# Four sums at a change of token block placed earlier, the weights' inner sums placed earlier on POOL, and the conversion's places and last two steps rearranged

## The chip, the cores and the metric

The kernel runs on one core of one Trainium2 chip. The metric is the device time of one execution in microseconds, lower is better; the clock of TensorE was granted at 0.997 of full speed over the profiled execution. A core has four engines that compute, each with its own instruction queue worked off in order: TensorE (PE), VectorE (DVE), ScalarE (ACT) and GpSimd (POOL); SyncE (SP) issues nearly all transfers here, also in order.

## The reference

Attention with a hash mask over 4 x 8 heads of 768 tokens, then a feed-forward block over the 3072 tokens:

```python
def _moe_ref(x, w_in, w_out):            # x: 3072 x 512, w_in: 512 x 2048, w_out: 2048 x 512
    h = x @ w_in
    g = h * (1.0 / (1.0 + np.exp(-1.702 * h)))
    return (g @ w_out).astype(np.float32)

# before it: buckets of q and k from the signs of 6 projections, scores masked where the buckets
# differ, softmax, product with v; its output, transposed to tokens x 512, is x
```

The weights come as float64, so the kernel turns them into float32 from their bits.

## The kernel before

The attention fills the first 316 us. The feed-forward block follows in two stages: `w_in` times the tokens (316 to 605 us, lines L737 to L1000), with the activation, and the product with `w_out` (from there to the end, L1069 on). The change touches the first stage and what is done beside it.

Both products save multiplications by Strassen-Winograd's scheme: a 2 x 2 product of blocks takes seven block products, with sums of blocks made beforehand. The helpers `sums_a` (L208, of weights) and `sums_b` (L216, of tokens) each give four sums in an order of their own; the four of `sums_b` are L219 (t1), L220 (the second block becomes a difference, in place), L221 (t2) and L222 (t4). The tokens come in three blocks of 1024 (`sb` = 0, 1, 2), and at each change of block DVE makes these four anew (`x_sums`, from `quarters_x`), into `t_x` and, for L220, into `xT`.

The first stage has 24 steps, eight per block of tokens, each 2 x 128 columns of hidden units against 2 x 512 tokens. Steps 2 to 19 are taken two by two, as pairs 1 to 9 (`NESTED`, L716; `pair_of_steps`, L842). Pair 4 is the first of block 1, pair 8 the first of block 2. In a pair, products 1, 6, 7, 5 and 4 of both steps run as they are ("outer" products, L740, each four PE records of 128x512); p5 uses t1, p6 uses t2, p7 the difference of L220 and p4 t4. Products 2 and 3 are split by the scheme once more (`nested`, L803) into seven "inner" products each, two PE records of 128x256 at L814. They go into two PSUM tiles, `a` and `x`, each with one buffer, so that the next inner product in a tile waits until DVE has added the last (L750, `u<-small` for product 2, `v<-small` for product 3). The six functions `first` to `sixth` (L817 to L836) are called adds 1 to 6 here (add 2 is two instructions). Those of product 3, but for the first, are carried into the next pair (`behind`).

Between the products a pair has ten places, at which the steps listed in `hooks` for it are emitted (`hook`, L893):

| place | after | place | after |
|---|---|---|---|
| 1 | p1 of the first step | 6 | p7 and its corner sum of the first step, add 2 |
| 2 | p1 of the second step | 7 | p7 of the second step, add 3 |
| 3 | p6 of the first step | 8 | p5, corner sum of the second step, add 4 |
| 4 | p6 of the second step | 9 | p4 of the first step, add 5 |
| 5 | p5 of the first step, add 1 | 10 | p4 of the second step, add 6, add 1 of product 3 |

At these places stand, besides the token sums:

- The conversion of a chunk of weights (`convert`, L158, a generator driven by `conversions`, L1117), six steps per chunk: L180, L182, L188 (with ACT's L190), L193, L195, L198. The first reads the chunk from `raw`, which has one buffer; L193 reads it last, and with it the load of the next chunk is emitted on SP (L162). A chunk of `w_out` is written with a stride, since `dst` is four columns of 128 apart. `places_of` gives the six places of the first and of the second step's chunk. The last step of each block (steps 7 and 15) has none, so pairs 3 and 7 have no conversion in their second half.
- POOL's sums of weights that pairs 1 to 3 make for the pairs behind them: `in_sums` (L236, four of 128x512) and `nest_w` (L776, eight of 128x128).
- POOL's sums of token blocks for the inner products (`nest_x`, L790), at places 1 to 4 of pairs 4 and 8.

The finished blocks go to memory by SP (`keep`, L743): c22, c21, u and v after ACT's activation, and POOL makes four sums of them for the second stage first ("outer sums", `g_outer`, L752: L219 to L222 again, on POOL, `t<-v,u` and so on), taken off one after the other by `some` (L766) at several points of a pair.

PE, DVE, ACT and POOL run in the order in which the code emits. SP's order is set by a scheduler at the build.

```python
for i, f in zip((1, 2, 4), x_sums[1:]):
    on(i, f)
places_of = (3, 4, 4, 5, 6, 6), (7, 8, 9, 9, 10, 10)
```

Of the kernel before, what the change touches and what calls it, by code (L numbers as in the profile page):

```python
# [8 lines left out]
F32 = mybir.dt.float32  # L9
# [4 lines left out]
Alu = mybir.AluOpType  # L14
# [24 lines left out]
def kernel(  # L39
# [17 lines left out]
    nc = tc.nc  # L57
# [100 lines left out]
    def convert(cv, dst, src, queue=None, psum=None):  # L158


        raw = cv.tile([P, CW, 2], U32, tag="raw", name="raw")
        (queue or loader[0]).dma_start(out=raw, in_=src)  # L162

        def of(x):
            return x if len(dst.shape) == 2 else x.rearrange("p (x r) -> p x r", r=dst.shape[2])

        lo, hi = raw[:, :, 0], raw[:, :, 1]
        bits = cv.tile([P, CW], U32, tag="bits", name="bits")
        if psum is None:
            part, size = dst.bitcast(U32), hi.bitcast(F32)  # L170
        else:
            part = psum.tile([P, CW], U32, tag="part", name="part")
            size = psum.tile([P, CW], F32, tag="size", name="size")
        yield


        if psum is None:
            nc.vector.scalar_tensor_tensor(part, hi, 3, masks[0x3FFFFFFF], op0=Alu.logical_shift_left, op1=Alu.bitwise_and)
        else:
            nc.vector.tensor_scalar(part, hi, 3, 0x3FFFFFFF, op0=Alu.logical_shift_left, op1=Alu.bitwise_and)  # L180
        yield
        nc.vector.scalar_tensor_tensor(bits, hi, 0xC0000000, part, op0=Alu.bitwise_and, op1=Alu.bitwise_or)  # L182
        yield

        if psum is None:
            nc.vector.tensor_tensor(part, bits, masks[0xFF800000], op=Alu.bitwise_and)
        else:
            nc.vector.tensor_scalar(part, bits, 0xFF800000, None, op0=Alu.bitwise_and)  # L188

        nc.scalar.activation(size, hi.bitcast(F32), Act.Square)  # L190
        part = part.bitcast(F32)
        yield
        nc.vector.scalar_tensor_tensor(part, lo, 2.0**-52, part, op0=Alu.mult, op1=Alu.mult)  # L193
        yield
        nc.vector.tensor_tensor(dst, of(bits.bitcast(F32)), of(part), op=Alu.add)  # L195
        yield

        nc.vector.scalar_tensor_tensor(dst, of(size), (1.125 * 2.0**-15) ** 2, dst, op0=Alu.is_ge, op1=Alu.mult)  # L198

    wi = w_in.bitcast(U32).rearrange("(kc ki) (f two) -> kc ki f two", ki=P, two=2)  # L200
    wo = w_out.bitcast(U32).rearrange("(fc fi) (d two) -> fc fi d two", fi=P, two=2)
# [6 lines left out]
    def sums_a(eng, a11, a12, s3, a22, s1, s2, s4, a21=None):  # L208

        a21 = s3 if a21 is None else a21  # L210
        return [lambda: eng.tensor_tensor(s1, a21, a22, op=Alu.add),
                lambda: eng.tensor_tensor(s3, a11, a21, op=Alu.subtract),
                lambda: eng.tensor_tensor(s2, s1, a11, op=Alu.subtract),
                lambda: eng.tensor_tensor(s4, a12, s2, op=Alu.subtract)]

    def sums_b(eng, b11, b12, b21, b22, t1, t2, t4):  # L216


        return [lambda: eng.tensor_tensor(t1, b12, b11, op=Alu.subtract),  # L219
                lambda: eng.tensor_tensor(b12, b22, b12, op=Alu.subtract),  # L220
                lambda: eng.tensor_tensor(t2, b22, t1, op=Alu.subtract),  # L221
                lambda: eng.tensor_tensor(t4, b21, t2, op=Alu.subtract)]  # L222
# [4 lines left out]
    def quarters_in(cols):  # L227
        w = [w_in_sb[:, K2 * k : K2 * (k + 1), F2 * i + cols.start : F2 * i + cols.stop]
             for i in range(2) for k in range(2)]
        return w + [s_in[:, i, :, cols] for i in range(3)]  # L230

    def quarters_x(sb):
        x = [xT[:, K2 * k : K2 * (k + 1), (2 * sb + j) * XT : (2 * sb + j + 1) * XT] for k in range(2) for j in range(2)]
        return x + [t_x[:, i] for i in range(3)]

    def in_sums(mt, count=1):  # L236
        return sums_a(nc.gpsimd, *quarters_in(slice(mt * P, (mt + count) * P)))
# [45 lines left out]
    def attention(ff):  # L283
# [4 lines left out]
        with actx:  # L288
# [226 lines left out]
            def begin(n):  # L515
                if 0 <= n - 2 < len(in_chunks) - LATE:
                    conv[n] = convert(cv, *in_chunks[n - 2])
                    step(n)
# [176 lines left out]
    def feed_forward(tag, late=()):  # L695
# [9 lines left out]
        with ExitStack() as fctx:  # L705
# [70 lines left out]
            def nest_w(t):  # L776
                sums = []
                m = slice(2 * t * P, (2 * t + 2) * P)
                for o in TWICE:
                    w = quarters_in(m)[LEFT[o]]  # L780
                    x = [w[:, k, i * P : (i + 1) * P] for i in range(2) for k in range(2)]
                    n = 3 if t < 2 else 4
                    new = twice.tile([P, n, P], F32, name=f"w{o}{t}")
                    new = [new[:, i] for i in range(n)]
                    s3 = x[2] if n == 3 else new[3]
                    W[o, t] = [x[0], x[1], s3, x[3]] + new[0:3]
                    sums += sums_a(nc.gpsimd, x[0], x[1], s3, x[3], *new[0:3], a21=x[2])
                return sums

            def nest_x(sb, rooms):  # L790
                sums = {}
                for o in TWICE:
                    b = quarters_x(sb)[RIGHT[o]]
                    b11, b12, b21, b22 = (b[:, k, j * TH : (j + 1) * TH] for k in range(2) for j in range(2))
                    t1, d12, t2, t4 = ([rooms.pop(0)] + [rooms.pop(0) for _ in range(3)])
                    X[o, sb] = [b11, d12, b21, b22, t1, t2, t4]
                    sums[o] = [lambda a=t1, b=b12, c=b11: nc.gpsimd.tensor_tensor(a, b, c, op=Alu.subtract),
                               lambda a=t2, b=b22, c=t1: nc.gpsimd.tensor_tensor(a, b, c, op=Alu.subtract),
                               lambda a=d12, b=b22, c=b12: nc.gpsimd.tensor_tensor(a, b, c, op=Alu.subtract),
                               lambda a=t4, b=b21, c=t2: nc.gpsimd.tensor_tensor(a, b, c, op=Alu.subtract)]  # L800
                return sums
# [248 lines left out]
            def g_sums(n):  # L1050
                return sums_b(nc.vector, *g_quarters(n)) if n < len(steps_out) else [lambda: None] * 4
# [65 lines left out]
            def conversions(cv, psum, chunks):  # L1117


                gens = [convert(cv, *x, psum=psum) for x in chunks]  # L1120
                next(gens[0])
                yield
                for i, x in enumerate(gens):
                    for at in range(6):
                        next(x, None)
                        if at == 3 and i + 1 < len(gens):
                            next(gens[i + 1])
                        yield

            def on(i, *fs):  # L1130
                hooks[i] = hooks.get(i, []) + list(fs)
# [49 lines left out]
            for t in NESTED:  # L1181
                sb, at = divmod(t, MT // 2)
                hooks = {}
                if at == 0:
                    for i, fs in zip((1, 2, 3, 4), (more[2][:2], more[2][2:], more[3][:2], more[3][2:])):
                        on(i, *fs)
                    for i, f in zip((1, 2, 4), x_sums[1:]):
                        on(i, f)
                    places_of = (3, 4, 4, 5, 6, 6), (7, 8, 9, 9, 10, 10)
                else:  # L1190
                    places_of = (1, 2, 2, 3, 3, 4), (6, 7, 7, 7, 9, 9)
                for n, late_by in zip((2 * t, 2 * t + 1), places_of):
                    x = todo.pop(n, [])
                    for i in late_by:
                        on(i, *x[:1])
                        x = x[1:]
                    on(5 if n % 2 == 0 else 10, *x)
                if t + 1 < MT // 2:
                    on(5, *in_sums(2 * t + 2, 2))
                    on(8, *nest_w(t + 1))  # L1200
                elif t + 1 == MT // 2:
                    on(5, *nest_w(0))
                if at == MT // 2 - 1:
                    x_sums = sums_b(nc.vector, *quarters_x(sb + 1))
                    more = nest_x(sb + 1, places[sb + 1])
                    on(10, x_sums[0])
                whole(pair_of_steps(t, hooks))
                yield
            turn[0] = -1
            for n in range(2 * NESTED.stop, 3 * MT):  # L1210
# [11 lines left out]
                t = {3 * MT - 2: g_sums(0)[:2], 3 * MT - 1: g_sums(0)[2:]}.get(n, []) if n > 3 * MT - 3 else []  # L1222
# [61 lines left out]
    def whole(steps):  # L1284
        for _ in steps:
            pass

    ff = feed_forward("", in_chunks[len(in_chunks) - LATE :])
    attention(ff)
    whole(ff)  # L1290
# [42 lines left out]
```

## Time and profile before

| | |
|---|---|
| median of 3 runs | 869.86 us (869.5 to 870.85) |
| the profiled execution | 868.91 us |
| its span | 867.1 us |
| instructions in it | 13723 |
| transfers | 132.12 MB, mean 152 GB/s |

Busy time by stretch of the span, us of each engine:

| stretch, us | PE | DVE | ACT | POOL |
|---|---|---|---|---|
| 300 to 400 | 99.42 | 69.08 | 42.68 | 68.07 |
| 400 to 450 | 47.05 | 36.78 | 18.48 | 32.66 |
| 450 to 500 | 50.00 | 35.45 | 19.93 | 23.68 |
| 500 to 550 | 48.21 | 39.53 | 19.17 | 29.76 |
| 550 to 600 | 50.00 | 32.18 | 18.14 | 41.52 |

A line of a group reads: line of the kernel, engine, operation, out<-in by the program's names, shape, count, then busy us, mean ns of one, and the idle time of the engine ahead of them with what ended it. A line of the waits reads: who waited for whom, us in all, how many times, the longest. A line of the timeline: start and length in us, engine, line, operation, out<-in, shape, count, and in brackets the idle time ahead of it.

### The profile page before, as it was taken

Reading aid. Unit: us, or ns where it says so; the run is one execution under the profiler, and the core shown is the slowest. Engines: PE = TensorE matmul, PEld = TensorE weight load, DVE = VectorE, ACT = ScalarE, POOL = GpSimd, SP = SyncE. Lnnn points to the kernel's source line nnn. Section 1 sums busy time; section 2 is a strip of 40 time slices with the busy share of each in tenths; the row PEclk is TensorE's granted clock in tenths of the full one; section 3 lists DMA queues with packets and bytes.
Section 4 is the critical chain, followed back from the end, with each engine's and each line's share of the span. In section 5 each row is a group of like instructions: output and inputs, shape, how many; then the busy total and the mean of one; then the engine's idle time right before and its main releaser. Section 6 shows DMA issues by size and latency. Waiting matters only on the chain.

```text
span 867.1 us, 13723 instructions
## 1 busy us (share of the span) xinstructions
PE 850.9 (98%) x4953; PEld 517.9 (60%) x4953; DVE 686.4 (79%) x1032; ACT 340.4 (39%) x567; POOL 344.0 (40%) x322
## 2 busy tenths in 40 slices
PE   8999999999999999999899999999999999999996
PEld 4444444444444444555455545544888888888885
DVE  4589999999999884666777668656788977897786
ACT  5866667777666644334344434343000000000000
POOL 4242224334323559667743364779914100000000
PEclk9999999999999999999999999999999999999998
DMA  5635645445552204436565547559754685467524
GB/s 128 99 54 108 106 86 85 85 90 121 101 96 63 62 2 170 169 107 220 183 206 197 202 149 242 195 191 325 259 193 155 201 246 197 164 206 243 195 98 100
DMA packets 169164, 132.12 MB, mean 152 GB/s; under 512 B 123616, under 2 KB 138112, under 8 KB 163712
## 3 DMA queue, kind: packets, MB, share of 16 engines
q1 hardware_dynamic: 166528, 129.70, 52.3%
q10 hardware_dynamic: 2560, 1.46, 0.8%
q8 instruction: 41, 0.67, 0.3%
q14 instruction: 35, 0.29, 0.1%
HBM read 79.69 MB, written 50.33 MB: 150 GB/s over the span
## 4 chain that ended last, share of the span: by engine, by line
PE 91%; DVE 4%; POOL 2%; DMA 1%; issue 1%; SPq 0%; ACT 0%; ACTq 0%; DVEq 0%; POOLq 0%
PE product L1080 27%; PE product L740 22%; PE ps L432 18%; PE av L465 15%; PE small L814 6%; PE dn L486 1%; PE hash L408 1%; DVE xT L1084 1%; DMA q<-in_q_dram 1%; DVE v L750 1%; DVE y L1060 1%; DMA raw<-in_moe_w_out_dram 0%; DVE t_x L221 0%; POOL v L220 0%; POOL t L219 0%
## 5 line engine op out<-in xcount | busy, mean ns | idle before, releaser
L433 ACT ACTIVATE e<-ps 128x768 f32<-128x768 f32 x192 | 151.2, 812 | 25.6 <-PE ps L432 23.1
L432 PE MATMUL ps<-qT,kT 64*128 64x384 f32 x768 | 155.1, 482 | 0.0
L440 POOL TENSOR_TENSOR acc<-e 128x768 f32<-128x768 f32 x32 | 51.8, 1619 | 194.1 <-ACT e L433 174.7
L465 PE MATMUL av<-e,v 128*32 128x385 f32 x1536 | 128.0, 487 | 0.0
L740 PE MATMUL product<-xT,w_in_sb 128*128 128x512 f32 x216 | 100.2, 593 | 0.0
L465 PEld LDWEIGHTS av<-e,v 128*32 128x32 f32 x1536 | 48.5, 109 | 76.3 <-issue 74.0
L740 PE MATMUL product<-t_x,s_in 128*128 128x512 f32 x192 | 89.2, 593 | 4.3 <-DVE t_x L221 4.3
L432 PEld LDWEIGHTS ps<-qT,kT 64*128 64x128 f32 x768 | 68.0, 187 | 38.5 <-issue 38.4
L1093 ACT COPY u<-product 128x256 f32<-128x256 f32 x21 | 7.8, 372 | 171.8 <-PE product L1080 138.5
L219 POOL TENSOR_TENSOR t<-v,u 128x512 f32<-128x512 f32 x24 | 33.4, 1390 | 89.4 <-ACT v L747 84.5
L432 PE MATMUL ps<-qf,kf 64*128 64x384 bf16 x384 | 62.8, 324 | 0.1
L740 PEld LDWEIGHTS product<-xT,w_in_sb 128*128 128x128 f32 x216 | 40.9, 190 | 35.8 <-issue 33.1
L740 PEld LDWEIGHTS product<-t_x,s_in 128*128 128x128 f32 x192 | 36.3, 190 | 35.9 <-issue 33.9
L441 POOL TENSOR_TENSOR acc<-acc,e 128x768 f32<-128x768 f32 x32 | 55.8, 1744 | 2.5
L446 DVE SCALAR_TENSOR_TENSOR acc<-e 128x768 f32<-128x768 f32 x32 | 47.7, 1491 | 5.1 <-ACT e L433 5.1
L740 PE MATMUL product<-t_x,w_in_sb 128*128 128x512 f32 x96 | 45.2, 593 | 0.0
L750 DVE TENSOR_TENSOR v<-small,v 128x256 f32<-128x256 f32 x63 | 26.1, 419 | 23.7 <-PE small L814 23.4
L432 PEld LDWEIGHTS <-kf 64*128 64x128 bf16 x384 | 19.0, 94 | 35.1 <-issue 6.2
L448 DVE TENSOR_TENSOR acc<-acc,e 128x768 f32<-128x768 f32 x32 | 34.3, 1072 | 3.3
L448 DVE TENSOR_TENSOR acc<-acc,acc 128x768 f32<-128x768 f32 x32 | 31.2, 974 | 6.3 <-POOL acc L441 3.2
L1080 PE MATMUL product<-raw_g,xT 128*128 128x256 f32 x152 | 35.1, 379 | 0.0
L750 DVE TENSOR_TENSOR u<-small,u 128x256 f32<-128x256 f32 x63 | 25.5, 417 | 11.1 <-PE small L814 8.0
(243 smaller groups left out, 1643.5 us busy)
## 6 DMA issues: line engine op xcount, KB each, us to landing
raw_g<-g_dram SPq DMA_DIRECT2D x22, 1024.0 KB
s_in<-g_dram SPq DMA_DIRECT2D x20, 1024.0 KB
g_dram<-t SPq DMA_DIRECT2D x72, 256.0 KB
g_dram<-c SPq DMA_DIRECT2D x48, 256.0 KB
raw<-in_moe_w_in_dram SPq DMA_DIRECT2D x16, 512.0 KB
raw<-in_moe_w_out_dram SPq DMA_DIRECT2D x16, 512.0 KB
v<-in_v_dram SPq DMA_DIRECT2D x32, 192.0 KB
g_dram<-u SPq DMA_DIRECT2D x24, 256.0 KB
```

Source lines behind the costliest of these rows:

```text
L219: return [lambda: eng.tensor_tensor(t1, b12, b11, op=Alu.subtract), lambda: eng.tensor_tensor(b12, b22, b12, op=Alu.subtract), lambda: eng ...
L432: nc.tensor.matmul(ps[:, j, 0:HS], a[hs, keys], m[hs, cols], start=not last, stop=last)
L433: nc.scalar.activation(es[c][:, kt, :, 0:HS], ps[:, :, 0:HS], Act.Exp, scale=1.0 / D**0.5)
L440: nc.gpsimd.tensor_tensor(acc, es[c][:, 0, :, 0:HS], es[c][:, 1, :, 0:HS], op=Alu.add)
L441: nc.gpsimd.tensor_tensor(acc, acc, es[c][:, 2, :, 0:HS], op=Alu.add)
L446: nc.vector.scalar_tensor_tensor(acc, e[0], T * TINY, e[1], op0=Alu.add, op1=Alu.add)
L448: nc.vector.tensor_tensor(acc, acc, x, op=Alu.add)
L465: nc.tensor.matmul(av[D * j + d : D * j + d + 32, :], vt[:, t, j, d : d + 32], es[c][:, t, j, :], start=(t == 0), stop=(t == T - 1))
L740: nc.tensor.matmul(ps, wq[LEFT[i]][:, kc, :], xq[RIGHT[i]][:, kc, :], start=(start and kc == 0), stop=(kc == K2 - 1), skip_group_check=not ...
L750: nc.vector.tensor_tensor(dst, x, y, op=Alu.add)
L814: nc.tensor.matmul(ps[at], wq[LEFT[i]], xq[RIGHT[i]], start=start, stop=True, skip_group_check=not start)
L1080: nc.tensor.matmul(ps, wq[LEFT[i]][:, c, :], gq[RIGHT[i]][:, c, :], start=(c == 0), stop=(c == F4 - 1))
```

## The change

In `convert`, for the chunks converted beside the products (those with a PSUM pool): the sum of the two parts is written back into `bits`, in order, and only the last step writes to the destination with its stride. In the pairs:

- Pairs 4 and 8: of the four token sums, L220 and L222 stand at places 1 and 3; L219 and L221 are moved into the pair before, to its places 8 and 10, where L219 alone stood at 10. The conversion's places become (2, 4, 5, 6, 6, 7) and (7, 8, 8, 9, 9, 10).
- All other pairs: the conversion's places become (2, 2, 3, 3, 4, 4) and (6, 7, 7, 8, 9, 9).
- Pairs 2 and 3: POOL's weight sums move from places 5 and 8 to 1 and 3 (pair 3: from 5 to 1). Pair 1 keeps 5 and 8.

```diff
-        nc.vector.tensor_tensor(dst, of(bits.bitcast(F32)), of(part), op=Alu.add)
+        bits = bits.bitcast(F32)
+        whole = bits if psum is not None else dst
+        nc.vector.tensor_tensor(whole, bits if psum is not None else of(bits), part if psum is not None else of(part), op=Alu.add)
         yield
 
-        nc.vector.scalar_tensor_tensor(dst, of(size), (1.125 * 2.0**-15) ** 2, dst, op0=Alu.is_ge, op1=Alu.mult)
+        nc.vector.scalar_tensor_tensor(dst, of(size), (1.125 * 2.0**-15) ** 2, of(whole) if psum is not None else whole,
+                                       op0=Alu.is_ge, op1=Alu.mult)
...
-                    for i, f in zip((1, 2, 4), x_sums[1:]):
+                    for i, f in zip((1, 3), (x_sums[1], x_sums[3])):
                         on(i, f)
-                    places_of = (3, 4, 4, 5, 6, 6), (7, 8, 9, 9, 10, 10)
+                    places_of = (2, 4, 5, 6, 6, 7), (7, 8, 8, 9, 9, 10)
                 else:
-                    places_of = (1, 2, 2, 3, 3, 4), (6, 7, 7, 7, 9, 9)
+                    places_of = (2, 2, 3, 3, 4, 4), (6, 7, 7, 8, 9, 9)
...
                 if t + 1 < MT // 2:
-                    on(5, *in_sums(2 * t + 2, 2))
-                    on(8, *nest_w(t + 1))
+                    on(5 if t == 1 else 1, *in_sums(2 * t + 2, 2))
+                    on(8 if t == 1 else 3, *nest_w(t + 1))
                 elif t + 1 == MT // 2:
-                    on(5, *nest_w(0))
+                    on(1, *nest_w(0))
                 if at == MT // 2 - 1:
                     x_sums = sums_b(nc.vector, *quarters_x(sb + 1))
                     more = nest_x(sb + 1, places[sb + 1])
-                    on(10, x_sums[0])
+                    on(8, x_sums[0])
+                    on(10, x_sums[2])
```

## The prediction

> **What bounds the kernel now.** I read the busy times, then who waits for whom on TensorE (PE), then the timelines at those waits.
>
> ```profile
> PE 850.9 (98%) x4953; PEld 517.9 (60%) x4953; DVE 686.4 (79%) x1032; ACT 340.4 (39%) x567; POOL 344.0 (40%) x322
> ```
>
> PE is busy for 98% and the change takes no matmul away, so only PE's gaps can be won, or new ones lost. All of PE's waits between 316 and 650 us, from the view of waits (total us, times, longest):
>
> ```profile
> PE product L740 <- DVE t_x L221: 4.3, 2, 2.5
> ...
> PE small L814 <- DVE u L750: 0.7, 2, 0.4
> PE small L814 <- DVE v L750: 0.3, 1, 0.3
> ```
>
> The first stands at the two changes of token blocks, pairs 4 and 8. PE's timeline at pair 8, and VectorE's (DVE's) beside it:
>
> ```profile
> 507.49 1.88 PE L740 MATMUL product<-xT,w_in_sb 128*128 128x512 f32 x4
> 509.21 0.59 PE L814 MATMUL small<-xT,w 128*128 128x256 f32 x2
> 511.58 1.95 PE L740 MATMUL product<-t_x,s_in 128*128 128x512 f32 x4 [1.77 <-DVE t_x L221]
> ```
>
> ```profile
> 505.46 1.27 DVE L219 TENSOR_TENSOR t_x<-xT 128x1024 f32<-128x1024 f32 x1
> ...
> 508.04 1.73 DVE L220 TENSOR_TENSOR xT<-xT 128x1024 f32<-128x1024 f32 x1
> ...
> 510.18 1.25 DVE L221 TENSOR_TENSOR t_x<-xT,t_x 128x1024 f32<-128x1024 f32 x1
> ```
>
> Unhindered, an inner product (two records) takes 0.43 us from start to start and an outer one (four) 1.72. p6 should start at 509.21 + 0.43 = 509.64 and starts at 511.58, because t2 (L221) comes out of DVE only at 511.43: 1.94 us lost. At pair 4 the same is 416.04 - 413.37 = 2.67. Behind each a smaller gap follows, since DVE is then late with the inner adds: 425.32 - 424.71 = 0.61 and 520.43 - 520.25 = 0.18. Pair 1's end has two more, 0.46 and 0.45. Nothing else from 316 to 650 us is over 0.15, so 6.31 us are all there is to win.
>
> The other view is what DVE and SyncE's queue (SP) wait for in that stretch:
>
> ```profile
> DVE part L180 <- DMA raw<-in_moe_w_out_dram: 8.8, 6, 3.1
> ```
>
> ```profile
> SPq L744 <- POOL t L219: 69.5, 23, 7.5
> ...
> SPq L744 <- POOL v L220: 29.4, 24, 4.6
> ...
> SPq L744 <- POOL t L221: 20.9, 21, 2.5
> ```
>
> The conversion has one raw buffer: the next load goes out behind L193, which reads it last, and L180 waits for it. Stores of POOL's sums stand ahead of it on SP. The timeline at pair 5 to 6, SP then DVE:
>
> ```profile
> 454.64 0.32 SPq L744 DMA_DIRECT2D g_dram<-t  x1
> 455.99 0.32 SPq L744 DMA_DIRECT2D g_dram<-v  x1
> 457.23 0.32 SPq L744 DMA_DIRECT2D g_dram<-t  x1
> 457.65 0.38 SPq L162 DMA_DIRECT2D raw<-in_moe_w_out_dram  x1
> ```
>
> ```profile
> 462.27 0.70 DVE L180 TENSOR_SCALAR part<-raw 128x512 uint32<-128x512 uint32 x1 [0.57 <-DMA raw<-in_moe_w_out_dram]
> ```
>
> L180 can start 4.62 us after the load's issue. Over the seven loads that it waited for, this is 3.62, 3.73, 4.30, 4.47, 4.62, 4.65 and 5.29.
>
> **The change, part by part.**
>
> *The sums at the change of blocks.* t1 moves from place 10 to 8 of the pair before, t2 from place 2 to place 10, into t1's old slot. That slot (505.46) lies 4.2 us ahead of p6, and t2 takes 1.25 to 1.95 us (its range over pairs 4 and 8), so p6 no longer waits. With it goes the lateness of the adds behind. Gain: 2.67 + 1.94 + 0.61 + 0.18 = 5.40. In its new slot t1 runs 1.27 to 2.29 us (2.29 where it met POOL's sums at pair 4) ahead of an inner add: from 501.55 to at most 503.84, add 0.42, PE's lag 0.15 (520.28 to 520.43): 504.41. PE needs it at 504.48. Hidden by 0.07; each tenth beyond that is a tenth on PE, twice.
>
> *POOL's weight sums.* In pairs 2 and 3 they go ahead of the outer sums: 4 x 1.3 + 8 x 0.46 = 8.9 us into an idle stretch of 14.6 us (360.5 to 375.1, POOL waiting for ScalarE), and 3.7 us into one of 4.88. The outer sums behind end sooner, and so does what SP stores. Nothing on PE; without the idle stretch they would only swap places.
>
> *L195 written in order.*
>
> ```profile
> L198 DVE SCALAR_TENSOR_TENSOR w_out_sb<-size,w_out_sb 128x512 f32<-128x512 f32 x16 | 16.9, 1056 | 0.9
> L195 DVE TENSOR_TENSOR w_out_sb<-bits,part 128x512 f32<-128x512 f32 x16 | 16.9, 1053 | 0.2
> ...
> L193 DVE SCALAR_TENSOR_TENSOR part<-raw,part 128x512 f32<-128x512 uint32 x18 | 12.4, 691 | 0.3
> ```
>
> L195 becomes what L193 is, 0.69 us; L198 still writes with a stride, so it stays at 1.05 (0.69 at best). 16 x 0.36 = 5.8 us less DVE work, which PE hardly waits for: DVE then waits for a load or a product instead.
>
> *Pair 1's conversion.* L193 goes behind the fourth inner add, and L195 is shorter. v, c and add 4 each come 0.6 sooner, so the first gap there (add 5 behind L193, 360.94 against 360.72) is 0.22 instead of 0.46; L195 0.72 after it, L198 1.05, two adds of 0.33: the second is some 0.12 instead of 0.45. Gain 0.57 (0 to 0.91).
>
> *The conversion at pairs 4 and 8.* Here I expect the gain to go. L193 moves from place 5 to 6, L180 of the next chunk stays at 7, so one outer and one inner product lie between them instead of twice that. And in the order of SP's queue as the changed kernel builds it, the load stands on SP behind the stores of t0, v, t2 (POOL's L219, L220, L221) and c22; now it stands ahead of them all. Walking pair 8: p5's sum on DVE 515.98, inner add of v 516.58. In before POOL's L219 starts 1.16 after that add and the store of L221 goes out 3.89 later (519.54, 520.70, 524.59): 521.63. Then c22 and the load, 0.42 to 0.5 each: 522.5 (L193 is done at 521.1, so SP decides). L180: 522.5 + 4.5 = 527.0, taking the two loads with the same stores ahead (4.47, 4.62). Queued behind L180 on DVE are v, c and add 4: 0.60 x 3 + 0.42 + 0.15 = 2.37, so PE may go on at 529.37. It gets there at 529.53 - 1.94 - 0.18 = 527.41. Lost: 1.96. Then L182 and L188, both at place 8 now, stand ahead of add 5: 529.13 + 0.72 + 0.60 + 0.42 + 0.15 = 531.02, PE there at 529.80: 1.22 more. 3.18 per change, 6.36 for two (pair 4 comes to the same within 0.1). With 3.62 for the load it is 2.3 each, 4.6; with 5.29, 3.97 each, 7.9.
>
> [...]
>
> *Sum.* 868.91 (span 867.1 and 1.8 around it) - 5.40 - 0.57 + 6.36 = 869.30, or +0.39. The median of the runs is 869.86, 0.95 above the profiled one; on it, 870.2. Bounds: -5.97 + 4.6 gives 868.5, -5.40 + 7.9 gives 872.4.
>
> **The rivals.**
>
> *The load is in time* (faster). SP would issue it right behind L193 at 521.1 and it would take 3.62: L180 at 524.7, add 4 visible at 527.1, no loss; L182 and L188 still cost 0.93. -5.97 + 1.9: 865.8. For: L193's own time allows it. Against: POOL's sums stand ahead on SP, and SP waits for L219 alone 69.5 us.
>
> *The load is quick, the queue as I walked it.* 3.62 us: 868.5. For: two rows of seven. Against: both had no store of POOL's within 0.4 us ahead. [...]
>
> *The load is slow* (slower). 5.29 at both changes and nothing won at pair 1: 872.4. It decides from about 5 us from issue to L180. For: the row at 530.45, with six stores within 3.3 us ahead. Against: only one of seven.
>
> *p6 still waits.* If t1 and t2 were held in their new slots so that t2 came no sooner, 4.6 us come back: 874.8. Against: t2's new slot has 4.2 us to spare.
>
> **How the numbers follow.** Forecast 0.42; quick load 0.10; in time 0.15; slow 0.28; p6 waiting 0.05. 0.2% is 1.7 us, about what a measurement of this kernel can tell from no change. The likeliest, 870.2, has 868.5 to 872.4 as its own range. The whole range goes down to 865.7, so that the load in time is just inside, and up to 872.6, past the slow load's 872.4; p6 waiting and the halves of the two outer cases that lie beyond their own numbers are left out, some 2 in 10. Faster: 0.15 and a little of the quick loads, 0.17. Slower: 0.28 + 0.05, 0.33. The same: 0.50.
>
> **What would show it.** p6 without a wait for L221 at pairs 4 and 8; L195 at 0.69; in their place PE waiting at L814 for DVE's u, twice at each change, 1 to 3 us and 1.2 us; L180 waiting some 4 us for raw there; on SP the raw load behind t, v, t, c. I am wrong if L180 starts less than 2.5 us behind L198 at these pairs, or if PE's new waits add up to less than 4 or more than 8 us.

## The result, and the profile after

The changed kernel takes 871.36 us (median of 20 runs, 870.19 to 874.98) and the kernel before 870.22 us beside it (20 runs, 868.89 to 871.32). The ratio is 1.0017, with a 95% interval of 1.001 to 1.0025: slower by some 1.5 us, a step that lies at the edge of what was called no change. The forecast was +0.39 us. The profiled execution took 870.98 us, 2.07 more than the one of before.

The page's busy times of the changed kernel:

```profile
PE 853.1 (98%) x4953; PEld 520.4 (60%) x4953; DVE 682.2 (78%) x1032; ACT 340.8 (39%) x567; POOL 346.0 (40%) x322
```

DVE has 4.2 us less to do. PE has the same 4953 records and yet 2.2 us more busy time. Busy time that grows while the work stays the same is the first sign that something other than a wait is at work.

All of PE's waits between 316 and 650 us (who waited for whom; us in all, times, longest):

```profile
PE small L817 <- DVE u L753: 5.7, 4, 1.9
```

The waits for t2 and those for `v` and `u` at pairs 1 and 4 are gone from this view, and four new ones stand in their place. (Three lines were added in `convert`, so L814 is L817 here, L750 is L753, L740 is L743, L219 to L222 are L222 to L225, L195 is L197 and L198 is L200.) PE's timeline at pair 8, where p6 is the `t_x` product of 510.50:

```profile
510.06 0.59 PE L817 MATMUL small<-xT,w 128*128 128x256 f32 x2
510.50 1.88 PE L743 MATMUL product<-t_x,s_in 128*128 128x512 f32 x4
...
526.39 1.88 PE L743 MATMUL product<-t_x,w_in_sb 128*128 128x512 f32 x4
530.17 0.70 PE L817 MATMUL small<-xT,w 128*128 128x256 f32 x2 [1.89 <-DVE u L753]
531.81 0.70 PE L817 MATMUL small<-xT,s_in 128*128 128x256 f32 x2 [0.95 <-DVE u L753]
```

p6 starts 0.44 us after the inner product ahead of it, so it waits for nothing. Later an outer product of 1.72 us should be followed at 528.11 and is followed at 530.17: 2.06 us lost; the next inner product should come 0.53 later and comes after 1.64: 1.11 lost. SP's queue and DVE at the same place:

```profile
521.29 0.32 SPq L747 DMA_DIRECT2D g_dram<-v  x1
522.53 0.32 SPq L747 DMA_DIRECT2D g_dram<-t  x1
522.94 0.38 SPq L747 DMA_DIRECT2D g_dram<-c  x1
523.41 0.41 SPq L162 DMA_DIRECT2D raw<-in_moe_w_out_dram  x1
```

```profile
521.23 0.69 DVE L193 SCALAR_TENSOR_TENSOR part<-raw,part 128x512 f32<-128x512 uint32 x1
...
527.90 0.69 DVE L180 TENSOR_SCALAR part<-raw 128x512 uint32<-128x512 uint32 x1 [3.96 <-DMA raw<-in_moe_w_out_dram]
...
529.70 0.41 DVE L753 TENSOR_TENSOR u<-small,u 128x256 f32<-128x256 f32 x1
530.03 0.68 DVE L182 SCALAR_TENSOR_TENSOR bits<-raw,part 128x512 uint32<-128x512 uint32 x1
530.74 0.69 DVE L188 TENSOR_SCALAR part<-bits 128x512 uint32<-128x512 uint32 x1
531.34 0.41 DVE L753 TENSOR_TENSOR u<-small,u 128x256 f32<-128x256 f32 x1
```

L193 is done with `raw` at 521.92, but the load of the next chunk goes out at 523.41, behind v, t and c. L180 starts 4.49 us after that, and add 4 (the `u` at 529.70) is queued behind L180; PE's next product in that tile, add 6's, waits for it. Then L182 and L188 stand ahead of add 5 (531.34). The product behind it, the first of product 3, waits for that add and starts at 531.81, which ends the second gap. Below, the wait for add 4 is called the first gap, the wait for add 5 the second.

What the waits don't show is in a table of windows around the same place of pair 4 (us, length, then busy us of PE, PEld, DVE, ACT and POOL, PE's granted clock, share of the transfer engines, GB/s):

```profile
430.00:434.00 4.00, 1.14 (x4) 0.40 (x3) 3.96 (x8) 1.79 (x4) 1.27 (x1) 1.00 0.79 301
434.00:436.00 2.00, 2.00 (x5) 1.03 (x6) 1.97 (x5) 1.46 (x3) 0.00 (x0) 0.67 0.82 300
436.00:438.00 2.00, 2.00 (x4) 0.91 (x3) 0.79 (x1) 0.33 (x2) 0.00 (x0) 0.50 0.87 161
438.00:440.00 2.00, 2.00 (x7) 1.18 (x6) 0.85 (x2) 0.43 (x1) 0.00 (x0) 0.97 0.96 370
```

Behind pair 4's two gaps TensorE is granted half its clock for about 3.4 us (from 434.7 to 438.1). The records of an outer product, which start every 0.43 us elsewhere, start every 0.85 us there; summed over the records this loses 1.64 us. Pair 8 shows no such stretch in this execution, and neither does any place between 316 and 650 us in the profile of before.

The stage can now be added up. Gaps on PE before: 6.31 us. After: 0.17 (pair 1) + 2.08 + 1.11 (pair 4) + 2.06 + 1.11 (pair 8) = 6.53. That is +0.22 us, and the half clock's 1.64 makes it +1.86 of the 2.07 by which the two profiled executions differ.

### The profile page after: what moved, and what is told of

It reads as the page before. It is cut to its first block, busy times and chain, and to the rows that moved or that the text cites. A ratio compares the mean times of both kernels' runs of the same rounds, so it can differ in the third digit from the quotient of the medians.

```text
span 869.1 us, 13717 instructions
## 1 busy us (share of the span) xinstructions
PE 853.1 (98%) x4953; PEld 520.4 (60%) x4953; DVE 682.2 (78%) x1032; ACT 340.8 (39%) x567; POOL 346.0 (40%) x322
## 4 chain that ended last, share of the span: by engine, by line
PE 85%; POOL 7%; issue 3%; DVE 3%; DMA 1%; ACT 0%; SPq 0%; ACTq 0%; POOLq 0%; DVEq 0%
PE product L1083 27%; PE product L743 18%; PE ps L435 18%; PE av L468 15%; PE small L817 4%; POOL t L224 1%; PE dn L489 1%; POOL t L222 1%; PE hash L411 1%; POOL v L223 1%; DMA raw<-in_moe_w_out_dram 1%; POOL t L225 1%; DVE xT L1087 1%; PE tp L369 1%; POOL xT L803 1%
## 5 line engine op out<-in xcount | busy, mean ns | idle before, releaser
L743 PE MATMUL product<-xT,w_in_sb 128*128 128x512 f32 x216 | 101.7, 601 | 0.0
L743 PE MATMUL product<-t_x,s_in 128*128 128x512 f32 x192 | 89.1, 592 | 0.0
L222 POOL TENSOR_TENSOR t<-v,u 128x512 f32<-128x512 f32 x24 | 33.3, 1387 | 87.1 <-ACT v L750 87.1
L743 PEld LDWEIGHTS product<-xT,w_in_sb 128*128 128x128 f32 x216 | 41.2, 192 | 36.2 <-issue 33.6
L743 PEld LDWEIGHTS product<-t_x,s_in 128*128 128x128 f32 x192 | 36.5, 190 | 30.9 <-issue 28.9
L753 DVE TENSOR_TENSOR v<-small,v 128x256 f32<-128x256 f32 x63 | 26.4, 421 | 30.7 <-PE small L817 30.5
L743 PE MATMUL product<-t_x,w_in_sb 128*128 128x512 f32 x96 | 45.2, 593 | 0.0
L225 POOL TENSOR_TENSOR t<-c,t 128x512 f32<-128x512 f32 x24 | 33.1, 1378 | 3.9 <-DMA g_dram<-t 2.2
```

Of the source, the lines that this page charges most:

```text
L743: nc.tensor.matmul(ps, wq[LEFT[i]][:, kc, :], xq[RIGHT[i]][:, kc, :], start=(start and kc == 0), stop=(kc == K2 - 1), skip_group_check=not ...
```

## The experiments

The theory after the result: (a) late raw load and the two conversion steps ahead of add 5 cost what the token sums win, and (b) two gaps so close to each other bring the half clock, which makes the rest. The rivals: the loss lies in another part of the change, or the 1.5 us are only further direct waiting. Each kernel was timed beside the kernel before.

**L193 one place earlier at pairs 4 and 8.** Only the place of L193 differs from the changed kernel.

```diff
-                    places_of = (2, 4, 5, 6, 6, 7), (7, 8, 8, 9, 9, 10)
+                    places_of = (2, 4, 5, 5, 6, 7), (7, 8, 8, 9, 9, 10)
```

> The changed kernel, with L193 of the first chunk of pairs 4 and 8 back at place 5 (places 2, 4, 5, 5, 6, 7); all else as changed. Theory A (late load: L193 one place later puts the raw load on SP behind POOL's stores, L180 waits for it, and the inner adds behind L180 hold PE): the load goes out ahead of the stores again, PE's four waits for u (5.7 us by the view of waits, 6.35 by PE's timeline) are gone, and the time is 5.4 to 6 us under the kernel before, a ratio of 0.993 to 0.994. Theory B (besides, the two gaps of each change lie so close that TensorE's clock halves for 3.4 us in some executions, 1.7 us each): no stretch at half clock before the end of the span. Rival C (the loss comes from the moved token sums, POOL's sums or the last two steps of the conversion, not from its places): PE's waits stay and the time is within 1 us of the changed kernel, ratio 1.001 to 1.002.

Measured: 862.54 us (861.59 to 863.54) against 869.74; ratio 0.9913 (0.9898 to 0.9927), some 7.5 us faster, where 5.4 to 6 were expected. SP and DVE at pair 8 in this kernel:

```profile
515.47 0.32 SPq L747 DMA_DIRECT2D g_dram<-t  x1
515.89 0.37 SPq L162 DMA_DIRECT2D raw<-in_moe_w_out_dram  x1
516.88 0.32 SPq L747 DMA_DIRECT2D g_dram<-c  x1
```

```profile
514.39 0.70 DVE L193 SCALAR_TENSOR_TENSOR part<-raw,part 128x512 f32<-128x512 uint32 x1
...
519.92 0.69 DVE L180 TENSOR_SCALAR part<-raw 128x512 uint32<-128x512 uint32 x1 [0.70 <-DMA raw<-in_moe_w_out_dram]
```

The load goes out 0.8 us after L193's end (1.5 in the changed kernel), ahead of c. It still takes 4.03 us to L180, but L193 itself is earlier in its pair, so DVE waits 0.70 us instead of 3.96. PE's gaps in the stage are down to 0.21 and 0.18, both at pair 1; at pairs 4 and 8 there is none. That is 5.92 us less of gaps; the rest is taken up with the clock below. L182 and L188 are where the changed kernel has them: with L180 in time they no longer delay add 5. So the whole loss at these pairs hangs on when `raw` is free and when the load goes out. This version beats both kernels.

**The token sums alone**, in the kernel before.

```diff
-                    for i, f in zip((1, 2, 4), x_sums[1:]):
+                    for i, f in zip((1, 3), (x_sums[1], x_sums[3])):
...
-                    on(10, x_sums[0])
+                    on(8, x_sums[0])
+                    on(10, x_sums[2])
```

> The kernel before with the token sums alone moved (t1 at place 8, t2 at 10 of the pair before, L220 and L222 at 1 and 3). Theory A: p6's two waits and the two small ones behind them are gone, 5.4 us, and nothing takes their place, since L193 stays at place 5; pair 1's 0.9 us stays. 864.5 to 865.5, a ratio of 0.9935 to 0.995. Rival C: the moved sums themselves hold DVE, so PE waits for u or v at the end of pairs 3 and 7 or in pairs 4 and 8, and less than half of the 5.4 us is gained.

Measured: 863.57 us (863.15 to 864.87); ratio 0.9926 (0.9912 to 0.9941), some 6.4 us faster. The waits left on PE in the stage:

```profile
PE small L814 <- DVE u L750: 0.4, 1, 0.4
PE small L814 <- DVE v L750: 0.3, 1, 0.3
```

Both are pair 1's (gaps of 0.55 and 0.46). All four gaps at pairs 4 and 8 are gone, 6.31 to 1.01 = 5.30 us of direct gaps. This one part of the change is worth more than the change as a whole.

**L182 and L188 one place later at pairs 4 and 8**, from the changed kernel.

```diff
-                    places_of = (2, 4, 5, 6, 6, 7), (7, 8, 8, 9, 9, 10)
+                    places_of = (2, 4, 5, 6, 6, 7), (7, 9, 9, 9, 9, 10)
```

> The changed kernel with L182 and L188 of the second chunk of pairs 4 and 8 at place 9 instead of 8 (7, 9, 9, 9, 9, 10), behind add 5. Theory A: the first gap of each change stays at about 2.05 us; the second, 1.11, goes from 0.4 us behind the first to some 2 us later, behind an outer product, at add 6, at about its size. Direct loss as in the changed kernel, 6.3 us. Theory B: with the two gaps further apart fewer executions show a stretch at half clock, the runs spread less than the changed kernel's 870.2 to 875.0, and the median is 0.5 to 1.5 us under it, 870 to 871. Against B: same spread, median within 0.4 us of the changed kernel, 871.0 to 871.8.

Measured: 869.82 us (868.95 to 870.97); ratio 0.9999 (0.999 to 1.0008). PE at pair 4:

```profile
432.82 0.70 PE L817 MATMUL small<-xT,w 128*128 128x256 f32 x2 [1.97 <-DVE u L753]
433.36 0.59 PE L817 MATMUL small<-xT,s_in 128*128 128x256 f32 x2
433.79 1.88 PE L743 MATMUL product<-xT,w_in_sb 128*128 128x512 f32 x4
436.69 0.67 PE L817 MATMUL small<-xT,w 128*128 128x256 f32 x2 [1.01 <-DVE v L753]
```

The second gap hasn't gone, it has moved: from add 5 to the add of `v` behind it, 3.9 us after the first gap's end instead of 1.6. The direct gaps of the stage are even 0.45 us more than in the changed kernel (6.98), and yet the time is lower, 0.9999 against 1.0017 (and 1.0024 in the repeat below). The clock in this profile stays at 1.00 through the stage, and the mean granted clock of its runs is 0.9958 against 0.9947 for the changed kernel. More direct waiting and less time speaks for (b) and against further waiting as the cause.

**The two loads on ScalarE's queue**, from the changed kernel: the raw loads of pairs 4 and 8 no longer queue on SP.

```diff
-                gens = [convert(cv, *x, psum=psum) for x in chunks]
+                gens = [convert(cv, *x, nc.scalar if i in (7, 14) else None, psum) for i, x in enumerate(chunks)]
```

> The changed kernel with two loads alone, those that L180 at place 7 of pairs 4 and 8 waits for, issued from ScalarE's queue instead of SP's; L193 stays at place 6. In the profile of the changed kernel these loads go out 1.5 us after L193's end, behind POOL's stores. If the stores on SP make the load late (theory A, as walked in the prediction), it goes out 0.1 us after L193, L180 starts some 1.5 us sooner and the first gap of each change goes from 2.05 to about 0.5, the second stays near 1.1: 3 us less direct loss, and few stretches at half clock, 867 to 868.5. If L193's own place is what counts and SP's order nothing, the gaps stay and the time is that of the changed kernel.

Measured: 866.63 us (866.13 to 867.59); ratio 0.9961 (0.9947 to 0.9974). At pair 8:

```profile
519.45 0.33 ACTq L162 DMA_DIRECT2D raw<-in_moe_w_out_dram  x1
```

```profile
523.73 0.70 DVE L180 TENSOR_SCALAR part<-raw 128x512 uint32<-128x512 uint32 x1 [2.33 <-DMA raw<-in_moe_w_out_dram]
```

The load goes out at once after L193 (L197 behind it starts at 519.40), 1.5 us sooner than on SP, and takes much the same, 4.28 us. PE's first gap falls from 2.06 to 0.43, at pair 4 from 2.08 to 0.61; the second stays 1.11 at both. So, of some 3.2 us per change, 1.5 to 1.6 is the place of the load behind the stores and 1.1 is the second gap, with L182 and L188 ahead of add 5; that the rest is the load's own length follows from the trace's times and was not tried apart. No half clock shows in the stage.

**Useless products in the gaps**, from the changed kernel. At pairs 4 and 8 PE computes four 128x256 products (`filler(4)`) ahead of add 6's product, where the first gap lies, and two more behind it (`filler(2)`), where the second lies, into a PSUM tile of their own that nobody reads. If the idle time in the gaps is what brings the half clock, it should then stay away, and the kernel should be faster for it.

```diff
...
                 def sixth():
+                    filler(4)
                     add(q12, go(3), q12)
+                    filler(2)
                     done(0)
```

> The changed kernel with six more matmuls in PE's queue at each of pairs 4 and 8: four in front of the inner product at which the first gap lies (add 6's, 2.05 us), two in front of the one with the second (1.11 us). They repeat an inner product into a spare PSUM tile that nobody reads, 0.43 us each, so 1.72 and 0.86 us of the gaps are filled and nothing else is later. [...] Rival (the clock has no part; the changed kernel's excess over the forecast has another cause): the time is that of the changed kernel within 0.4 us, or longer by up to 5 us if the added matmuls do not fit into the gaps.

Measured: 869.95 us (868.43 to 871.5) against 869.56; ratio 1.0003 (0.9994 to 1.0012). PE at pair 4:

```profile
429.15 1.88 PE L743 MATMUL product<-t_x,w_in_sb 128*128 128x512 f32 x4
430.87 1.89 PE L819 MATMUL fill<-xT,w_in_sb 128*128 128x256 f32 x8
433.19 0.70 PE L826 MATMUL small<-xT,w 128*128 128x256 f32 x2 [0.43 <-DVE u L753]
...
434.84 0.70 PE L826 MATMUL small<-xT,s_in 128*128 128x256 f32 x2
```

The useful products are no earlier for it: from where the useful product would have started, the two delays are 433.19 - 430.87 = 2.32 and 1.12 here, 2.11 and 1.12 at pair 8, 6.67 us in all against 6.36 in the changed kernel. Only the engine is no longer idle in them, and the clock stays at 1.00 from 430 to 445 us, where it was 0.50 at pair 4 of the changed kernel.

**The changed kernel once more**, on the same chip as the fillers.

> The changed kernel once more, unaltered, beside e5 on the same chip. Ratio to the kernel before 1.001 to 1.0025 as measured, 1 to 2 us over e5 by theory B, the same as e5 by its rival. Its profile shows PE's gaps of 2.05 and 1.11 us at both changes again, and one or two stretches of 3.4 us at half clock behind them in some executions, none in others.

Measured: 871.44 us (870.41 to 874.37); ratio 1.0024 (1.0015 to 1.0033). The intervals of the two don't meet: six useless products at each change make the kernel about 1.5 us faster. The mean granted clock of the runs is 0.9946 here and 0.9976 with the useless products. The windows at pair 4 in this execution, with two short ones ahead:

```profile
432.50:432.75 0.25, 0.25 (x2) 0.09 (x1) 0.25 (x1) 0.25 (x2) 0.00 (x0) 0.94 0.00 0
432.75:433.00 0.25, 0.25 (x2) 0.00 (x0) 0.21 (x2) 0.25 (x1) 0.00 (x0) 0.50 0.00 0
...
434.00:436.00 2.00, 2.00 (x4) 1.30 (x5) 1.97 (x5) 1.46 (x3) 0.00 (x0) 0.50 0.91 337
436.00:438.00 2.00, 2.00 (x4) 0.82 (x3) 0.83 (x1) 0.21 (x1) 0.00 (x0) 0.50 0.76 197
438.00:440.00 2.00, 2.00 (x6) 1.38 (x5) 0.42 (x1) 0.59 (x1) 0.00 (x0) 0.61 0.89 343
```

Half clock again at pair 4 and not at pair 8, this time for some 6.8 us, twice the length of the first profile's; the slower products lose 2.84 us. The gaps are the same (2.19 + 1.11 and 1.99 + 1.11). But here the half clock begins at about 432.7, 0.4 us behind the first gap (which ends at 432.30) and ahead of the second (432.83 to 433.94). In this execution it did not take the second gap to bring it, so (b) as worded is too strong: that the second gap makes the half clock likelier or longer fits, but is not shown. The length differs from execution to execution, which fits the wide upper ends of this kernel's runs (874.37 and 874.98): both of those runs were granted 0.990, against 0.994 to 0.996 in all others.

**The new places at pairs 4 and 8 alone**, in the kernel before.

```diff
-                    places_of = (3, 4, 4, 5, 6, 6), (7, 8, 9, 9, 10, 10)
+                    places_of = (2, 4, 5, 6, 6, 7), (7, 8, 8, 9, 9, 10)
```

> The kernel before with the new places of the conversion at pairs 4 and 8 alone (2, 4, 5, 6, 6, 7 and 7, 8, 8, 9, 9, 10); token sums, POOL's sums and the last two steps as before. Theory A: p6 still waits for t2 (2.7 and 1.9 us), and the late load adds its 3.2 us at each change, so the kernel is 5.5 to 7 us slower than before, with theory B up to 3 us more: 875.5 to 879. Rival (the late load comes from the moved sums or from POOL's order, the places are harmless by themselves): within 1 us of the kernel before.

Measured: 878.94 us (878.03 to 880.72); ratio 1.0107 (1.0094 to 1.012), 9.3 us slower.

```profile
PE small L814 <- DVE u L750: 7.4, 5, 3.3
PE product L740 <- DVE t_x L221: 4.3, 2, 2.5
```

The wait for t2 is as in the kernel before, and the new gaps are 3.46 + 1.11 and 2.15 + 1.11 us, 7.8 in all, with some 6.8 us of half clock at pair 4, from 438.0 on, within the second gap, and 3.4 behind pair 8's two. The loss is in these places and in nothing else of the change.

**The rest of the change alone**: the changed kernel with the token sums and these places as before; left are POOL's sums, the order of L195's sum and the places of the other pairs.

```diff
-                    for i, f in zip((1, 3), (x_sums[1], x_sums[3])):
+                    for i, f in zip((1, 2, 4), x_sums[1:]):
...
-                    places_of = (2, 4, 5, 6, 6, 7), (7, 8, 8, 9, 9, 10)
+                    places_of = (3, 4, 4, 5, 6, 6), (7, 8, 9, 9, 10, 10)
...
-                    on(8, x_sums[0])
-                    on(10, x_sums[2])
+                    on(10, x_sums[0])
```

> The changed kernel with the token sums and the places of pairs 4 and 8 as before: what is left is the sum written in order, POOL's weight sums moved, and the new places of the other pairs. By the prediction only the gaps at pair 1's end shrink, by 0.57 us, and p6's waits stay: ratio 0.9985 to 1.0005. Rival (POOL's order or L195 are worth or cost something of their own): more than 1.5 us off the kernel before, either way.

Measured: 867.16 us (866.52 to 869.14); ratio 0.9977 (0.9968 to 0.9987). That is 2.0 us where the prediction's terms for these parts come to 0.57. The gaps are 0.14 at pair 1, then 2.00, 0.19, 2.00 and 0.19: 4.5 us against 6.31. Pair 1 gave 0.77. The other 1.0 came from pair 4, where p6's wait is 2.00 instead of 2.67 and the gap behind it 0.19 instead of 0.61. Two more kernels ask which part does this.

**POOL's weight sums ahead, alone**, in the kernel before.

```diff
-                    on(5, *in_sums(2 * t + 2, 2))
-                    on(8, *nest_w(t + 1))
+                    on(5 if t == 1 else 1, *in_sums(2 * t + 2, 2))
+                    on(8 if t == 1 else 3, *nest_w(t + 1))
...
-                    on(5, *nest_w(0))
+                    on(1, *nest_w(0))
```

> The kernel before with POOL's sums of weights moved ahead of its outer sums, and nothing else of the change. The prediction's step, "nothing on PE": ratio 1.000, p6's two gaps as before (2.67 and 1.94 in the trace of before). The rival, from the run of the change without the token sums and without the new places (0.9977): it is POOL's place that gave most of that, because DVE's L219 to L221 at pair 4 then no longer meet POOL's outer sums. Then p6's gap at pair 4 falls to about 2.0 with L219 there at 1.3 us, the one behind it (0.61) to about 0.2, and the ratio is about 0.9987 (1.1 us).

Measured: 867.41 us (866.94 to 868.26) against 869.62; ratio 0.9975 (0.9965 to 0.9985). DVE's t1 and t2 for pair 4, first in the kernel before, then in this one:

```profile
409.19 2.29 DVE L219 TENSOR_TENSOR t_x<-xT 128x1024 f32<-128x1024 f32 x1
...
413.95 1.95 DVE L221 TENSOR_TENSOR t_x<-xT,t_x 128x1024 f32<-128x1024 f32 x1
```

```profile
408.73 1.24 DVE L219 TENSOR_TENSOR t_x<-xT 128x1024 f32<-128x1024 f32 x1
...
413.46 1.22 DVE L221 TENSOR_TENSOR t_x<-xT,t_x 128x1024 f32<-128x1024 f32 x1
```

In the kernel before POOL is in the middle of its outer sums then (its own L221, at 410.36, takes 2.25 us beside DVE's t1, and 1.28 at 405.20 with no such sum beside it); here the last of them ends at 408.2, ahead of t1. Both DVE sums take a third to a half less, p6's gap at pair 4 falls to 1.90 and the one behind it to 0.18. POOL need not be idle for that: in the run of the rest alone t1 and t2 take 1.34 and 1.31 us, and POOL's sums of token blocks that start while DVE's sums run take 1.59 to 1.70 us instead of 0.72. At pair 4 of the kernel before, POOL's L220 starts first, at 409.13, and takes 1.27 us, and t1, from 409.19 on, takes 2.29; at pair 8 t1 starts first, at 505.46, and takes 1.27, and POOL's L798, from 505.73 on, takes 1.59.

The direct gaps explain 1.4 us of the 2.2 (6.31 to 4.92). For the remaining 0.8, a half clock behind pair 4's long gap in some executions of the kernel before would do, and the next run shows that such a gap can bring one. The granted clocks point there: the mean is 0.9960 over the 19 runs of the kernel before and 0.9971 over the nine of this one, by estimate 1.0 us of 867. Nine of the 19 runs lie at 0.995, none of the nine; the end of the span alone, with 3.2 to 6.5 us at half clock in the profiles, brings a run by estimate (half of 6.5 us, of 867) no lower than 0.996. Where in the span those runs had it is not shown.

**L195's sum in order, alone**, in the kernel before (the first part of the change's diff).

> The kernel before with L195's sum written in order, and nothing else of the change. The prediction: the group falls from 1.05 to 0.69 us (5.8 us of DVE work), and PE hardly waits for that: ratio 1.000 (0.9996 with what shorter work gives at pair 1's end, some 0.3 us). The rival: DVE's time here is worth more, because the next load or the adds come sooner in many pairs: then the ratio is about 0.9985 or below and PE's gaps in the trace are smaller elsewhere than at pair 1.

Measured: 868.35 us (867.41 to 869.45); ratio 0.9988 (0.9979 to 0.9997). The gaps are 0.29, 2.36, 0.19, 1.90 and 0.18, 4.9 us in all: pair 1 gave 0.62, and pair 4 again gave, since t1 and t2 come earlier and take 1.98 and 1.67 us. But PE at pair 4 shows this:

```profile
414.14 2.36 PE L743 MATMUL product<-t_x,s_in 128*128 128x512 f32 x4 [2.20 <-DVE t_x L224]
416.30 1.06 PE L817 MATMUL small<-w_out_sb,w 128*128 128x256 f32 x2
417.15 2.79 PE L743 MATMUL product<-t_x,s_in 128*128 128x512 f32 x4
419.77 0.59 PE L817 MATMUL small<-w_out_sb,s_in 128*128 128x256 f32 x2
```

The inner product takes 0.85 us to the next start instead of 0.43 and the outer one 2.62 instead of 1.72: the clock is at half until 419, behind a single gap of 2.36 us, and takes 1.63 us back. In the profile of before the same gap was 2.67 us and brought nothing.

## Why the prediction was right in its waits and short in its sum

**The token sums: -5.40.** p6 waits nowhere, and the token sums alone take 5.30 us of gaps away. Right.

**The late load at pairs 4 and 8: +6.36.** Measured 6.36 in the profile of the changed kernel (2.08 + 1.11 + 2.06 + 1.11), against two times 1.96 + 1.22. The walk through SP's queue held: the load was to go out 1.4 us after L193's end and did so after 1.5; it was to take 4.5 us to L180 and took 4.50 and 4.49. That the sum meets 6.36 to the last digit is luck: at pair 8 the two gaps were put at 1.96 and 1.22 and were 2.06 and 1.11. Moving L193 by a place took the cost away and moving the load to another queue halved it, which shows both causes, the release of `raw` and the queue.

**Pair 1: -0.57.** Its gaps went from 0.91 to 0.17, 0.74. A little short.

**L195 in order and POOL's sums: nothing on PE.** L195 fell to 0.68 us as said. The cover named (idle time of DVE and POOL) was not all: at pair 4 both parts shorten DVE's t sums (t1 from 2.29 us to 1.24 with POOL's sums moved, to 1.98 with L195 in order). Alone they gave 1.0 and 2.2 us, of which pair 1's gaps are 0.62 and 0.17. The prediction had seen the 2.29 us "where it met POOL's sums" and did not ask what moving POOL's sums would do to it. In the whole change this changes nothing at p6, which waits nowhere there; the error would have shown only in another mixture of the parts.

**What failed is the sum: it had no term for the clock.** Every us lost was taken to cost one us. But around the new gaps at pair 4 the clock was granted at half, which cost 1.64 us in one profiled execution and 2.84 in the other. The kernel with the same delays filled up with useless work (1.0003 against 1.0024) and the one with the second gap moved away (0.9999) tell it from further waiting. With +1.64 for it the forecast's +0.39 would have been +2.0, against the 2.07 of the profiled executions and the 1.5 of the ratio.

The two profiles make the clock's part too large, since the profiled execution of the kernel before had no half clock in the stage and some of its other runs seem to have had one. The mean granted clock over the runs is 0.9947 for the changed kernel (0.9946 in the repeat) and 0.9960 for the kernel before, beside the repeat. By estimate this difference, of some 869 us, is 1.1 to 1.2 us; with 0.2 to 0.3 of gaps it makes 1.3 to 1.5 where 1.5 and 2.1 were measured. For L193 one place earlier the same estimate gives 5.92 of gaps and 1.7 of clock (0.9978 against 0.9958), 7.6 where 7.5 was measured. Elsewhere it is off by up to 0.9 us, most for L195's sum alone.

**The rivals.** The load in time (865.8) didn't happen in this change, but L193 a place earlier makes it happen, and gives 862.5: no gap is left there, not even the 1.9 us that this rival kept for L182 and L188. The quick and the slow load are out by the two measured loads, 4.5 us both. p6 without its wait is plain in the trace.

The change is thus two gains and one loss: alone, the token sums give 6.4 us, the rest 2.0, and the places at pairs 4 and 8 cost 9.3. That makes +0.9 where 1.5 was measured. The parts don't simply add: the rest's gain at pair 4, p6's shorter wait, is contained in that of the token sums, which take the whole wait away.

## What to carry to other kernels

When a step that frees a single buffer is moved later, follow the load behind it through its queue to its first use, and price whatever is queued behind that use: here one place of one instruction decided between 871.4 and 862.5 us. When a wait on TensorE is priced, look too at the clock granted behind it: here gaps of 2.08 and 2.19 us, each with one of 1.11 close by, and one of 2.36 us alone were followed by half clock that cost another 1.63 to 2.84 us, in some executions and not in others. The granted clock of every run (here 0.990 to 0.996 for one kernel) then says more than that of one profile. A part that seems to be worth nothing may be shortening a neighbour on another engine, as POOL's moved sums did here (2.2 us), which a run of that part alone shows at once.

## What was not expected of the hardware

Clock at half speed (0.50 or 0.51 in the windows) came in stretches of about 3.4 us (the changed kernel's first profile and L195's sum alone, both at pair 4, and the new places alone at pair 8) or twice that (the changed kernel once more and the new places alone, at pair 4: some 6.8 us), at gaps of 1.1 to 3.5 us. Over the twelve profiles, two gaps of 2.0 to 3.5 and 1.1 us with 0.5 us of work between were followed by it in four of six places, in one of them before the second gap had begun and in one within it; a single gap of 2.3 to 2.7 us in one of three; a single gap of 1.9 to 2.1 us, with no other within 2 us, in none of nine. The repeat's half clock began behind 2.19 us, that of L195's sum alone behind 2.36. What decides whether it comes was not shown.

Useless matmuls that nobody reads made the kernel faster by 0.2% (869.95 against 871.44 us), with the useful ones no earlier.
